# The complex sums and the way back of a spectral layer: sums over 128 partitions on GpSimd, products of 64 rows

## The chip, the cores and the metric

The kernel runs on one core of a Trainium2 chip. The metric is the device time of one execution, in microseconds (us). Before the change three runs gave 786.98, 787.42 and 789.71 us; the median is 787.42. The engines are called as in the profile: PE (TensorE matmul), PEld (its weight loads), DVE (VectorE), ACT (ScalarE), POOL (GpSimd) and SP (the queue that issues the DMAs).

## The reference

```python
def _A_ref(x, w_r, w_i):                 # spectral layer, S = 2048, D = 512
    X = rfft2(x); X = X * (w_r + 1j * w_i)
    return irfft2(X, s=(S, D))
def _B_ref(u, ...):                      # long convolution along S
    K = 2 * einsum("dn,dnl->dl", C, exp(A * dt * pos)).real
    y = irfft(rfft(u, 2 * L) * rfft(K, 2 * L))[..., :L]
    return y + u * D_skip
x = A_x
x = x + _A_ref(_layernorm(x), A_w_r, A_w_i)
x = x + _B_ref(_layernorm(x), ...)
x = x + _A_ref(_layernorm(x), A_w_r, A_w_i)
x = x + _B_ref(_layernorm(x), ...)
```

Everything is float32. The spectral layer (A) is a two-dimensional Fourier transform, a product with complex weights for each frequency, and the transform back. Layer B is a convolution whose kernel K (the "series") doesn't depend on x.

## The kernel before, in words

The transforms are matmuls with constant tables. A row index of 2048 is split into 128 x 16, and the 16 groups of frequencies are the steps `q` of a layer A (function `layer_a`). The layer has three lists of steps:

- `spread` (first layer) or `spread_four` (second layer): layer norm, sums and differences of the columns, and the first stage of the transform along the rows. The result is `ZA`.
- `middle`, for t = 0 to 17: `forward(t)`, `weigh(t-1)` and `back(t-2)`.
- `end`: `fold` and `rows_back`, the transforms back along columns and rows and the residual addition.

The change lies in `middle`, and there in these operations of each `q`:

- `forward` (lines 493 to 518): 4 matmuls of 128 rows and 128 weight columns (L497 to L501) into one bank; ACT copies the bank to the tile `z` in four pieces (L507, L511), two small places of which POOL has cleared (L503, L504). SP issues the DMA of the weights `W` (L513), and POOL patches two columns of them (L515).
- `weigh`: for each of the two parts `pl` (real, imaginary) a bank `px` gets two matmuls of 64 weight columns side by side, one for each half `v` of the frequencies (recorded as L316, the helper `side_by_side`). DVE multiplies it with both parts of the weights into `m[pl]` (L527, 128x514). Then the complex sums: real part = m[0][re] - m[1][im] (L532), imaginary part = m[1][re] + m[0][im] (L533), each for the half `v` of 64 partitions by itself, written so that in `Y` the real part lies in partitions 0 to 63 and the imaginary part in 64 to 127, with `v` as an index along the row. The strings `YA` (first layer) and `YA2` (second) name the engine of each of the four sums; g is POOL, v is DVE. One addition of 2 columns follows (L534, on POOL in the first layer, on DVE in the second).
- `back`: 4 matmuls (L545) with 128 columns of `Y` as weights, for both `v` and both `oe` (odd and even columns), each summing over the 128 partitions, real and imaginary together, into one bank; ACT copies the bank to `U[0]` and `U[1]` (L548), one copy for each `oe`.

The tag `u` is a pool of two buffers of 16 KB per partition. In turn it holds the rows of x of the first layer (`here`), the two halves of `U`, and in `layer_b` the tiles `Y` and `V`. PSUM has 8 banks; while the first layer runs, 5 of them are shared by `forward`, `weigh` and `back` (tags `p1`, `p2`, `p3`), in the second layer they have 2, 3 and 3. The tag `w` (7 buffers of 2 KB) holds `z`, `m` and `Y`, and in the second layer also the weights `W`.

Beside the first layer A runs `kernel_time`, the making of the series for layer B: 64 half units, each with matmuls (L825, L835, L836, L839, L870), exponentials and sines on ACT (L800), three kinds of DVE work (L838, L857, L859) and a product on POOL (L821, L822). Its steps are woven into the lists of the first layer A and of layer B in shares given by `FILL`, by the order in the program. A scheduler then orders the instructions of each engine by a timeline of its own and fills the gaps, so the order on an engine isn't that of the program text, and a change of one part can move others. Each engine works through its list in order. The second layer A has no series work beside it: its `middle` runs alone.

In layer B the function `weigh` multiplies the transformed rows by the transformed series (L962) and sums with L974, mostly on POOL.

## Time and profile before

| what | value |
|---|---|
| median of the runs | 787.42 us |
| span of the profiled execution, first to last instruction | 781.1 us |
| what lies around the span, by the median | 6.3 us |
| mean granted TensorE clock | 0.934 |
| bytes moved by DMA | 80.64 MB, mean 103 GB/s |

The profile is of one execution and gives its span; a separate whole time of that execution isn't recorded, so the 6.3 us are the median less the span. A line of a view names the place in the code (L545), the engine, the operation, what it writes and reads (the names of tiles), the size, and the count. A matmul of 32-bit numbers has two records, and each has a weight load of its own; "128*64" ahead of a size is the shape of the part of the array that the matmul uses, rows * columns. "[1.09 <-DMA wt]" is idle time of the engine ahead of the instruction, in us, and what ended it.

### The profile page before, as it was taken

What the parts mean: (1) busy time and instruction counts of PE and PEld (TensorE: products, weight loads), DVE (VectorE), ACT (ScalarE), POOL (GpSimd) and SP (SyncE); (2) the same over time, 40 slices, a digit from 0 to 9 for tenths busy, and PEclk for the clock granted to TensorE, in tenths of its full rate; (3) what the DMA queues carried; (4) which work ended last, traced back from release to release, by engine and by line L of the source; (5) the groups of instructions that cost most, each with busy time, mean ns of one, the idle gap of its engine ahead of it and who ended that gap; (6) DMA issues with size and microseconds to landing.
All of it is one profiled execution on the core that took longest, in us unless ns stands there. A gap on an engine that the chain in (4) does not pass through costs nothing. (4 is left out here: it accounts for less than half of the span.)

```text
span 781.1 us, 18929 instructions
## 1 busy us (share of the span) xinstructions
PE 627.7 (80%) x7248; PEld 443.5 (57%) x7248; DVE 649.3 (83%) x1301; ACT 428.1 (55%) x919; POOL 404.9 (52%) x596
## 2 busy tenths in 40 slices
PE   3447888897867977998889887874899896989986
PEld 2336666665534543656365656654777663566766
DVE  7998748979998999769996997878578696889992
ACT  3433778854748765887568834323756336242312
POOL 3675876764825245721657266281055572475760
PEclk9998899999979997999989999997999999799998
DMA  8300552344546503452325539422133114234513
GB/s 311 128 0 1 129 138 56 110 75 151 114 167 184 137 9 64 124 145 82 51 68 117 192 55 257 141 95 69 55 82 83 28 28 136 70 95 120 154 29 83
DMA packets 144923, 80.64 MB, mean 103 GB/s; under 512 B 78561, under 2 KB 124513, under 8 KB 143937
## 3 DMA queue, kind: packets, MB, share of 16 engines
q1 hardware_dynamic: 144576, 78.90, 36.2%
q8 instruction: 58, 0.95, 0.5%
q0 software_dynamic: 256, 0.52, 0.4%
q14 instruction: 33, 0.26, 0.1%
HBM read 54.89 MB, written 25.03 MB: 102 GB/s over the span
## 5 line engine op out<-in xcount | busy, mean ns | idle before, releaser
L974 POOL TENSOR_TENSOR u<-wb,wb 64x512 f32<-64x512 f32 x90 | 129.2, 1436 | 85.2 <-DVE wb L962 75.9
L316 PE MATMUL p<-z,mb 128*64 128x512 f32 (+2 forms) x480 | 102.0, 535 | 8.3 <-DVE wb L962 5.4
L870 PE MATMUL pv<-qp 128*64 128x128 f32 x1024 | 78.9, 295 | 11.4 <-DVE qp L859 6.9
L859 DVE TENSOR_TENSOR qp<-qp,mag 128x1024 f32<-128x1024 f32 x64 | 83.8, 1317 | 1.0
L962 DVE TENSOR_TENSOR wb<-p,kk 128x512 f32<-128x512 f32 x128 | 80.6, 674 | 4.7 <-PE p L316 4.6
L870 PEld LDWEIGHTS pv<-qp 128*64 128x64 f32 x1024 | 62.0, 147 | 38.8 <-ACT stage L878 10.2
L648 ACT COPY z<-p 128x512 f32<-128x512 f32 x96 | 51.4, 597 | 58.1 <-PE p L316 43.7
L316 PE MATMUL p<-mb,u 128*64 128x64 f32 x2048 | 72.9, 235 | 10.6 <-DVE u L974 4.5
L316 PEld LDWEIGHTS p<-mb,u 128*64 128x64 f32 x2048 | 70.7, 150 | 18.7 <-issue 11.3
L857 DVE SCALAR_TENSOR_TENSOR qp<-qp,mag 128x256 f32<-128x256 f32 x128 | 64.8, 523 | 13.6 <-ACT qp L800 13.3
L654 DVE STREAM_TRANSPOSE z<-z 128x512 f32<-128x512 f32 x96 | 58.5, 673 | 18.0 <-ACT z L648 18.0
L527 DVE TENSOR_TENSOR w<-wt,p 128x514 f32<-128x514 f32 x64 | 42.6, 686 | 33.3 <-PE p L316 18.6
L1086 POOL TENSOR_SCALAR w<-w,norms 128x128 f32<-128x128 f32 x64 | 40.5, 647 | 51.9 <-DMA w<-h 28.3
L532 POOL TENSOR_TENSOR w<-w,w 64x257 f32<-64x257 f32 x48 | 40.1, 835 | 50.3 <-DVE w L527 46.2
L456 PE MATMUL p<-w,w 128*128 128x128 f32 x128 | 32.0, 429 | 40.8 <-DVE w L449 30.8
L987 ACT COPY u<-p 128x512 f32<-128x512 f32 x64 | 37.6, 590 | 43.8 <-PE p L316 43.8
L316 PEld LDWEIGHTS p<-z,mb 128*64 128x64 f32 x480 | 34.2, 140 | 37.0 <-issue 20.2
L456 PEld LDWEIGHTS p<-w,w 128*128 128x128 f32 x128 | 27.8, 318 | 44.7 <-issue 24.8
L800 ACT ACTIVATE kf<-pk 128x512 f32<-128x512 f32 x64 | 38.9, 608 | 24.1 <-PE pk L839 23.6
L316 PE MATMUL p<-t,w 64*64 64x128 f32 x1024 | 43.3, 290 | 5.8 <-issue 2.6
L974 DVE TENSOR_TENSOR u<-wb,wb 64x512 f32<-64x512 f32 x38 | 46.9, 1234 | 0.5
L800 ACT ACTIVATE qp<-kf,half 128x512 f32<-128x512 f32 x64 | 47.2, 737 | 0.1
(200 smaller groups left out, 1495.3 us busy)
## 6 DMA issues: line engine op xcount, KB each, us to landing
wt<-in_w SPq DMA_DIRECT2D x32, 257.0 KB
kf<-kk SPq DMA_DIRECT2D x32, 256.0 KB
kk<-kf SPq DMA_DIRECT2D x32, 256.0 KB
u<-in_x SPq DMA_DIRECT2D x16, 256.0 KB
hr<-in_x SPq DMA_DIRECT2D x16, 256.0 KB
kt<-stage SPq DMA_DIRECT2D x32, 128.0 KB
h<-hr SPq DMA_DIRECT2D x16, 256.0 KB
w<-kt SPq DMA_DIRECT2D x32, 128.0 KB
```

Of the source, the lines that this page charges most:

```text
L316: last = self.nc.tensor.matmul(out, weights, data, start=not more, stop=True, skip_group_check=True).ins
L456: nc.tensor.matmul(p[:, b], xf[:, b], t, start=True, stop=True)
L527: nc.vector.tensor_mul(m[pl], W, px[:, None, :].to_broadcast([128, 2, 257]))
L648: nc.scalar.copy(tiles["z"][:, :, :, b, m:m + 2].rearrange("p u j m r -> p (u j) (m r)"), ps[b].rearrange("p u j m r -> p (u j) (m r)"))
L654: nc.vector.transpose(tiles["zt"][:, u:u + 8].rearrange("p u j d -> p (u j d)"), tiles["z"][:, u:u + 8].rearrange("p u j b m r -> p (u j b ...
L800: last["x"] = nc.scalar.activation(*a, **k).ins
L857: nc.vector.scalar_tensor_tensor(QP[:, c, 0], QP[:, c, 1, :, ::-1], -1.0 if c else 1.0, m[:, 0], op0=ALU.mult, op1=ALU.mult)
L859: nc.vector.tensor_mul(t, t, mag[:, None, 1:3, 256 * j:256 * j + 256].to_broadcast([128, 2, 2, 256]))
L870: nc.tensor.matmul(p[64 * t:64 * t + 64, g], QP[:, c, 2, d:d + 2].rearrange("p s a -> p (s a)"), QP[:, c, 0:2, d:d + 2].rearrange("p k s b ...
L962: nc.vector.tensor_mul(split(m[c, pl], "du", [32, 16]), by_channel(p), split(k[c], "du", [32, 16]))
L974: self.added = e[0].tensor_sub(y[0:64], v[0, 0], v[1, 1]), e[1].tensor_add(y[64:128], v[0, 1], v[1, 0])
L1086: (self.nc.gpsimd if XNE[k] == "g" else self.nc.vector).tensor_scalar(t[:, k], t[:, k], scale, bias, op0=ALU.mult, op1=ALU.add)
```

## The change

The sums run over all 128 partitions: `Y` now has the half `v` in the partitions, as `m` has it, and real and imaginary part side by side along the row. That makes two sums of 128x257 in place of four of 64x257, both on POOL in both layers. Since real and imaginary part are no longer in different partitions, `back` sums them by two matmuls of 64 rows that accumulate (`r` = 0 and 1), for each half `v` and each `oe`: 8 matmuls in place of 4, the two halves into two banks. ACT copies one bank for each `v`. The table `ST` for `back` is twice as long, so the constant tile `ca` has 256 columns more. `U`, `here`, and `Y` with `V`, each become one tile of 32 KB, and the tag `u` one buffer.

```diff
-YA = 'ggvg'
+YA = 'gg'
...
-YA2 = 'gvgv'
+YA2 = 'gg'
...
-    ca.append(MM.transpose(2, 3, 0, 1, 4).reshape(128, 256))
+    ca.append(np.broadcast_to(MM.transpose(3, 0, 2, 1, 4).reshape(64, 512), (2, 64, 512)).reshape(128, 512))
...
-        here = [self.sb("u", [8, 512]) for _ in range(2)] if x is None else []
+        here = self.sb("u", [16, 512]) if x is None else None
...
             Y = self.sb("w", [2, 257])
-            for v in range(2):
-                hs = slice(64 * v, 64 * v + 64)
-                e = [nc.vector if c == "v" else nc.gpsimd for c in ya[2 * v:2 * v + 2]]
-                e[0].tensor_sub(Y[0:64, v], m[0][hs, 0], m[1][hs, 1])
-                e[1].tensor_add(Y[64:128, v], m[1][hs, 0], m[0][hs, 1])
+            e = [adders[c] for c in ya]
+            e[0].tensor_sub(Y[:, 0], m[0][:, 0], m[1][:, 1])
+            e[1].tensor_add(Y[:, 1], m[1][:, 0], m[0][:, 1])
             adders[ye].tensor_add(Y[:, :, 128], Y[:, :, 128], Y[:, :, 256])
...
-                U.extend(self.sb("u", [2, 16, 16, 8]) for oe in range(2))
-            p = self.ps("p3", [2, 2, 128])
+                u = self.sb("u", [2, 2, 16, 16, 8])
+                U.extend((u[:, 0], u[:, 1], u))
+            p = [self.ps("p3", [2, 128]) for v in range(2)]
+            for oe in range(2):
+                for r in range(2):
+                    for v in range(2):
+                        hs = slice(64 * v, 64 * v + 64)
+                        nc.tensor.matmul(p[v][:, oe], Y[hs, r, 128 * oe:128 * oe + 128], k["ST"][hs, int(q + v > 0), r],
+                                         start=r == 0, stop=r == 1, skip_group_check=True)
             for v in range(2):
-                st = k["ST"][:, int(q + v > 0)]
-                for oe in range(2):
-                    nc.tensor.matmul(p[:, oe, v], Y[:, v, 128 * oe:128 * oe + 128], st, start=True, stop=True,
-                                     skip_group_check=True)
-            for oe in range(2):
-                nc.scalar.copy(U[oe].rearrange("p s n q (v c) -> p v (s n) q c", v=2)[:, :, :, q],
-                               p[:, oe].rearrange("p v (n c) -> p v n c", c=4))
+                nc.scalar.copy(U[2].rearrange("p o s n q (v c) -> p v o (s n) q c", v=2)[:, v, :, :, q],
+                               p[v].rearrange("p o (n c) -> p o n c", c=4))
...
-        Y, V = self.sb("u", [2, 32, 64]), self.sb("u", [32, 2, 2, 32])
+        YV = self.sb("u", [2, 4096])
+        Y, V = split(YV[:, 0], "abc", [2, 32, 64]), split(YV[:, 1], "abcd", [32, 2, 2, 32])
...
-                    net.phase("a", x=(32768, 1), ta=(8192, 1), ca=(6912, 1), u=(16384, 2), w=(2056, WA), wt=(2056, WT), hr="wt",
+                    net.phase("a", x=(32768, 1), ta=(8192, 1), ca=(7704, 1), u=(32768, 1), w=(2056, WA), wt=(2056, WT), hr="wt",
...
-            outer.enter_context(net.phase("b", t2=(8192, 1), u=(16384, 2), kk=(2048, 8), ta="t2", wt="w", wb="w", xw="w"))
+            outer.enter_context(net.phase("b", t2=(8192, 1), u=(32768, 1), kk=(2048, 8), ta="t2", wt="w", wb="w", xw="w"))
```

In the changed kernel the sums are lines 530 and 531, the small addition is line 532 and the matmuls of `back` are still line 545; behind `layer_b`'s first lines every line number is one higher.

More of the change, by code (lines that the diff above doesn't have):

```diff
@@ L393, in consts @@
         def consts():
-            C = self.load("ca", "ca", [CUTS[-1] + 512])
+            C = self.load("ca", "ca", [CUTS[-1] + 768])
             k["R"], k["Q"] = ([C[:, a:b] for a, b in zip(CUTS[i:i + 4], CUTS[i + 1:i + 5])] for i in (0, 4))
             k["S"] = split(C[:, CUTS[-1]:CUTS[-1] + 256], "abc", [2, 2, 64])
-            k["ST"] = split(C[:, CUTS[-1] + 256:CUTS[-1] + 512], "ab", [2, 128])
+            k["ST"] = split(C[:, CUTS[-1] + 256:CUTS[-1] + 768], "abc", [2, 2, 128])
         if x is not None:
@@ L419, in spread @@
                 G = starts[starts.index(n2) + 1] - n2
-                norm["rows"] = [row(k_, here[k_ // 8][:, k_ % 8]) for k_ in range(n2, n2 + G)]
+                norm["rows"] = [row(k_, here[:, k_]) for k_ in range(n2, n2 + G)]
                 if not S1:
@@ L1160, in switch @@
                 banks.enter_context(net.phase("pb", P, p1=(2048, PB[0]), p2=(2048, PB[1]), p3="p1"))
-                outer.enter_context(net.phase("h", side="right", za=(32768, 1), ca=(6912, 1), wv="kk", junk="kk"))
+                outer.enter_context(net.phase("h", side="right", za=(32768, 1), ca=(7704, 1), wv="kk", junk="kk"))
                 wide.enter_context(net.phase("wide", side="right", wb=(2048, WW), z3=(16384, 1), xw=(2048, 4)))
```

## The prediction

> I call the 16 steps of `middle` in the first spectral layer **Middle 1** (77 to 155 us) and those of the second **Middle 2** (561 to 616 us). A step holds one `forward`, one `weigh` and one `back`.
>
> **What bounds the kernel now.** First the page's busy times, then the busy time by stage (start and end, length, then busy us and instruction records of PE, PEld, DVE, ACT and POOL, granted clock, DMA share, GB/s).
>
> ```profile
> span 781.1 us, 18929 instructions
> PE 627.7 (80%) x7248; PEld 443.5 (57%) x7248; DVE 649.3 (83%) x1301; ACT 428.1 (55%) x919; POOL 404.9 (52%) x596
> ```
>
> ```profile
> 77.00:155.00 78.00, 67.20 (x505) 49.77 (x503) 57.78 (x82) 64.12 (x140) 55.75 (x116) 0.91 0.42 108
> 155.00:300.00 145.00, 118.53 (x1023) 71.39 (x1019) 129.75 (x294) 93.86 (x181) 72.66 (x101) 0.93 0.44 115
> 561.00:616.00 55.00, 50.76 (x384) 38.32 (x384) 40.91 (x80) 32.44 (x96) 28.53 (x74) 1.00 0.26 69
> ```
>
> No engine is the bound everywhere. In Middle 1 PE is busiest (67.2 of 78 us); from 155 to 300 us it is DVE (129.75 of 145); in Middle 2 it is PE again (50.76 of 55), with POOL at half. The weight loads in order of time show what one step of Middle 2 is made of.
>
> ```profile
> 589.78 0.30 PEld L497 LDWEIGHTS p<-ca,z 128*128 128x128 f32 x2 [0.39 <-issue]
> 590.67 0.97 PEld L545 LDWEIGHTS p<-ca,w 128*128 128x128 f32 x8
> 591.76 0.63 PEld L316 LDWEIGHTS p<-w,ca 128*64 128x64 f32 x8
> 592.78 0.30 PEld L497 LDWEIGHTS p<-ca,z 128*128 128x128 f32 x2 [0.39 <-issue]
> ```
>
> The step is 3.00 us long: 0.89 for `forward` (4 matmuls, 0.222 each), 1.09 for `back`, 1.02 for `weigh`, and PE waits for no engine in it. So Middle 2 is worth 16 x 3.0 = 48 us plus its beginning, its end and two stalls. `back` has 4 matmuls of the same form as `forward`, so about 0.88 of its 1.09 is streaming, and 0.21 is lost where the array goes over from 128*128 to 128*64. `weigh` has two pairs of matmuls of 257 columns, the halves of a pair side by side: `forward`'s columns (132, then three times 128) take 1.72 ns each, so 2 x 257 take 0.88, which leaves 0.14 for the way back to 128*128. **A change of the array's shape costs about 0.18 us.**
>
> By the Trainium skill, page "TensorEngine Tiling (Array Packing)", section "Key Properties", a change of tiling mode drains the engine. That speaks against this change, which brings in a third shape; the page has no price, and the 0.14 and 0.21 above agree with it.
>
> **The sums go to GpSimd.** The groups by line and shape (count, busy us, mean ns; the idle time is not needed) price the old and the new sums.
>
> ```profile
> L532 POOL TENSOR_TENSOR w<-w,w 64x257 f32<-64x257 f32 x48 | 40.1, 835 | 50.3 <-DVE w L527 46.2 <-ACT kf L800 1.6 <-ACT w L511 0.7
> L533 POOL TENSOR_TENSOR w<-w,w 64x257 f32<-64x257 f32 x32 | 21.4, 669 | 2.3
> L533 DVE TENSOR_TENSOR w<-w,w 64x257 f32<-64x257 f32 x32 | 18.8, 587 | 1.1
> L532 DVE TENSOR_TENSOR w<-w,w 64x257 f32<-64x257 f32 x16 | 10.3, 644 | 1.5 <-DVE w L527 0.5
> L1062 POOL TENSOR_TENSOR t<-za 128x512 f32<-128x512 f32 x8 | 11.1, 1419 | 0.1
> L974 POOL TENSOR_TENSOR u<-wb,wb 64x512 f32<-64x512 f32 x90 | 129.2, 1436 | 85.2 <-DVE wb L962 75.9 <-DVE wb L964 4.0
> L588 POOL TENSOR_TENSOR wv<-w 128x254 f32<-128x254 f32 x32 | 26.3, 823 | 0.8
> ```
>
> POOL takes as long for 128 rows as for 64 (1419 and 1436 ns at 512 columns), so a 128x257 sum is priced by the 128x254 row, 0.82 us; the ends are the 64x257 means, 0.67 and 0.84. DVE loses 16 sums of 0.644 in Middle 1 (10.3 us) and 32 of 0.587 in Middle 2 (18.8 us). POOL goes from 48 sums to 32 in Middle 1 and keeps 32 in Middle 2. Does the new pair of POOL sums delay Middle 2, where the adds ran on DVE beside them?
>
> ```profile
> 590.74 0.68 DVE L527 TENSOR_TENSOR w<-wt,p 128x514 f32<-128x514 f32 x1
> 591.46 1.35 DVE L533 TENSOR_TENSOR w<-w,w 64x257 f32<-64x257 f32 x2
> 591.70 0.23 POOL L515 COPY wt<-ends 128x4 f32<-128x4 f32 x1 [1.09 <-DMA wt<-in_w]
> 591.89 1.42 POOL L532 TENSOR_TENSOR w<-w,w 64x257 f32<-64x257 f32 x2
> ```
>
> The products are ready at 591.42. POOL's queue first holds the patch of the next weights (L515), which waits for their DMA; now both sums are behind it, not only the subtractions. From 591.89 two sums of 0.82 end at 593.5, and the 128x2 addition on DVE about 0.2 later, 593.7: that is when `back` is due in the old rhythm (590.67 + 3.00). So it fits exactly, and if PE's step becomes longer there is slack. DVE's 18.8 us in Middle 2 buys nothing, for DVE wasn't late; without the cover of a longer step each 0.1 us of delay would cost 16 x 0.1 = 1.6 us.
>
> **The way back as 64-row products.** Per step 8 matmuls of 64 rows x 128 columns take the place of 4 of 128 rows. Before has no 64x128 shape; the nearest is 64*64 in layer B.
>
> ```profile
> 686.02 0.86 PEld L316 LDWEIGHTS p<-t,x 64*64 64x64 f32 x32
> ```
>
> 32 records in 0.86 us are 0.027 each, against 0.111 for a record of 128*128 (two records to a matmul): four quarters of the array run at once, two of them row halves. So a 64-row product alone takes 0.22 us like a full one, and one of rows 0 to 63 with one of rows 64 to 127 takes 0.22 together. The source alternates the halves, which would be 4 slots of 0.22 per step, as now. But the scheduler's order in the changed kernel often doesn't alternate: in steps 3, 5, 7, 9 and 11 of Middle 2 it issues one upper-half product, a matmul of `forward`, then three upper and four lower; in steps 4, 6, 8, 10 and 12 one upper, a matmul of `forward`, and then lower and upper in turn. If a product starts no earlier than the one ahead of it in the queue, and each half runs one at a time, the 128 products of Middle 2 need 88 slots, where 64 are needed now, and those of Middle 1 86. The shape changes go from 34 to 66 in Middle 2 and from 44 to 73 in Middle 1, counted in the same two orders.
>
> Middle 2: 24 more slots x 0.22 = 5.3 us, 32 more changes x 0.18 = 5.8 us, together 11.1 us. Bounds: 0 if halves always overlap and the new changes are free; 64 x 0.22 + 32 x 0.20 = 20.5 if they never overlap.
>
> By the Trainium skill, page "TensorE: Matmul & The Clock Gate", section "Part 3: Packing small matmuls", matmuls start and end in program order; by that rule it is the 88 slots, while halves pulled forward past each other would make it 64 and the sum 5.3 us less. No row of before shows a run of one half followed by a run of the other.
>
> **What comes back.** Two steps of Middle 2 are longer than 3.00 because POOL's patch came late.
>
> ```profile
> 579.19 0.30 PEld L497 LDWEIGHTS p<-ca,z 128*128 128x128 f32 x2 [0.39 <-issue]
> ...
> 583.77 0.30 PEld L497 LDWEIGHTS p<-ca,z 128*128 128x128 f32 x2 [0.39 <-issue]
> ...
> 598.78 0.30 PEld L497 LDWEIGHTS p<-ca,z 128*128 128x128 f32 x2 [0.39 <-issue]
> ...
> 602.79 0.30 PEld L497 LDWEIGHTS p<-ca,z 128*128 128x128 f32 x2 [0.39 <-issue]
> ```
>
> They took 4.58 and 4.01 us, 2.6 more than two plain steps. With steps of about 3.7 us the weights have more time; I take 2.1 of the 2.6 as won. **Middle 2: 11.1 - 2.1 = +9.0 us.**
>
> **Middle 1 and the kernel's time series behind it.** Here `middle` is woven with units of `kernel_time`, whose DVE work is
>
> ```profile
> L859 DVE TENSOR_TENSOR qp<-qp,mag 128x1024 f32<-128x1024 f32 x64 | 83.8, 1317 | 1.0
> L857 DVE SCALAR_TENSOR_TENSOR qp<-qp,mag 128x256 f32<-128x256 f32 x128 | 64.8, 523 | 13.6 <-ACT qp L800 13.3
> L838 DVE TENSOR_SCALAR kw<-pk 128x512 bf16<-128x512 f32 x64 | 43.0, 677 | 1.7 <-PE pk L836 1.6
> ```
>
> 0.68 + 2 x 0.52 + 1.32 = 3.0 us for each of 64 half units. PE gets 22 slots x 0.22 + 29 changes x 0.18 = 10.1 us more, at the clock of 0.91 that this stage was granted 11.0 us, as much as all its idle time there (78 - 67.2 = 10.8). DVE gets 10.3 us less. The scheduler also moves series work back: at the end of Middle 1 DVE has done 4 half units where it had done 6, at the first `weigh` of layer B 24 where it had done 30; by that layer's 32nd weighting product both have 51, and from there to Middle 2 the orders are nearly the same. So if DVE sets the pace up to there, the stretch ends 10.3 us earlier; if PE does, 11.0 later. The rows above say PE for the first 78 us and DVE for the 145 behind it, and the half units that leave Middle 1 go to where DVE has little room (15 us in 145). What held DVE in Middle 1 is partly relieved:
>
> (waits from 80 to 152 us: total, times, longest)
>
> ```profile
> DVE w L527 <- POOL w L534: 8.8, 2, 6.1
> DVE w L527 <- PE p L316: 5.3, 4, 1.8
> ```
>
> but the longest of those waits, 6.1 us, is the 128x2 addition on POOL behind a series instruction that waits for ACT,
>
> ```profile
> 112.40 0.24 POOL L821 TENSOR_TENSOR e<-mag 128x16 f32<-128x16 f32 x1 [2.90 <-ACT mag L800]
> ```
>
> and in the changed kernel an L821 still stands ahead of that addition in the same step. The ends nearly cancel; I take **+1.0 us**, ends -10 and +11.
>
> **At no cost:**
>
> ```profile
> L548 ACT COPY u<-p 128x256 f32<-128x256 f32 x64 | 20.7, 374 | 9.7 <-PE p L545 9.6
> 17.63 0.33 SPq L305 DMA_DIRECT2D ca<-in_ca  x1
> 73.21 0.81 PE L497 MATMUL p<-ca,x 128*128 128x132 f32 x2 [0.46 <-ACT x L458]
> ```
>
> ACT's two copies per step keep their 256 elements; the 0.13 MB more of `ca` (256 columns x 128 rows x 4 bytes) are asked for at 18 us and needed at 73; the one 32 KB buffer makes `back`'s first write wait for all rows of the layer, and layer B's first write for all of the folds, both of which stand ahead in the data flow anyway. `back` takes two banks instead of one: with steps of 3 us or more its copies (0.37 us each) free them in time. From 616 us to the end the order is unchanged.
>
> **Sum.** 781.1 + 9.0 + 1.0 = 791.1 us of span. The median of the runs, 787.42, is 6.3 above the span, which I leave as it is: 797.4 us.
>
> **Rivals.**
> 1. *No overlap of the halves at all:* each runs alone. Middle 2 then costs 20.5 - 2.6 = 17.9, Middle 1 half of 64 x 0.22 + 29 x 0.20 = 20, so 10: 815 us. Against it: the 64*64 row.
> 2. *It cancels:* DVE's 10.3 us come off up to layer B, for it is the busiest engine behind Middle 1, and Middle 2 costs the 9.0: 786 us.
> 3. *Faster:* PE takes row halves without a drain and overlaps them whatever their order. Middle 2 then keeps its 3.0 us step (-1 for the stalls), and DVE's 10.3 us up to layer B lead, of which I count 8: 778 us. It decides if a change to 64*128 costs under 0.05 us and a step needs no more than 4.3 slots. Against it: the 0.21 behind every `back` now.
> 4. *GpSimd becomes the bound:* if a 128-row sum took twice a 64-row one, 1.43 us, POOL would need 2.9 and 0.2 for the patch per step, 3.1, still less than PE's 3.7: it adds nothing unless rival 3 holds. The L1062 row is against it.
>
> **Chances.** The forecast 0.66, rival 1 0.09, rival 2 0.14, rival 3 with 4 0.11. A measurement of this kernel tells apart about 0.5%, 3.9 us: faster 0.11, same 0.14, slower 0.75. The forecast's own range is 789 to 806: 7 either way for Middle 1, short of its ends, and 32 x 0.04 for the price of a shape change. For 8 in 10 it has to reach rival 2 and some way to rival 1: 785 to 810.
>
> **What would show it.** Middle 2's step by its L497 starts: 3.2 where the halves alternate, about 3.8 and 4.2 in the two other orders; all at 3.0 means rival 3, all above 4.3 rival 1. POOL's 128x257 near 0.8 us. L527 on DVE in Middle 2 waiting for PE, and PE for nobody. The 32nd L962 of layer B within some 5 us of its old time; 10 earlier would mean rival 2. I am wrong if PE waits for POOL in Middle 2, or if the series work shifts the stretch up to 300 us by more than 11.

## The result, and the profile after

The changed kernel takes **820.75 us** in the median of four runs (811.35 to 822.92), the kernel before 788.21 us beside it: a ratio of 1.041, 95% interval 1.034 to 1.048. It is slower, as forecast, but by 32 us, where 10 were forecast, and lies above the range of 785 to 810.

The page's busy times of the changed kernel, and the windows of the two stages ahead of 300 us and of the new Middle 2:

```profile
span 820.8 us, 19319 instructions
PE 654.5 (80%) x7504; PEld 457.4 (56%) x7504; DVE 619.0 (75%) x1253; ACT 430.1 (52%) x919; POOL 380.0 (46%) x580
```

```profile
77.00:155.00 78.00, 73.69 (x615) 52.77 (x612) 45.97 (x63) 58.98 (x132) 39.22 (x98) 0.93 0.41 107
155.00:300.00 145.00, 115.54 (x952) 68.80 (x951) 120.33 (x284) 83.82 (x163) 65.09 (x94) 0.87 0.42 112
589.00:652.00 63.00, 59.43 (x496) 43.81 (x496) 22.42 (x47) 32.99 (x96) 23.61 (x73) 1.00 0.22 60
```

From 77 to 155 us PE is busy for 73.69 us instead of 67.20, DVE for 45.97 instead of 57.78: more for PE and less for DVE, as the sum had it. Over the whole span PE is busy 27 us longer, DVE 30 us less. But from 155 to 300 us DVE, the bound of that stage before, does 9.4 us less work than before, and no engine does more. Work has been put off.

Where it went is seen in the first and last start of four groups of DVE instructions (their columns: count, shortest, median and longest ns, first and last start). L859 ends each half unit of the series; L601 is the residual addition that ends the first layer A; L962 (after: L963) is layer B's weighting; L527 in the second layer marks Middle 2. Before:

```profile
L601 DVE TENSOR_TENSOR hr<-hr,p x16: 647/672/687, 164.4 to 229.2; 128x512 f32<-128x512 f32 x16
L962 DVE TENSOR_TENSOR wb<-p,kk x64: 650/672/692, 284.5 to 517.0; 128x512 f32<-128x512 f32 x64
L859 DVE TENSOR_TENSOR qp<-qp,mag x64: 1185/1218/2301, 126.8 to 454.5; 128x1024 f32<-128x1024 f32 x64
L527 DVE TENSOR_TENSOR w<-wt,p x32: 681/690/692, 564.4 to 612.1; 128x514 f32<-128x514 f32 x32
```

After:

```profile
L601 DVE TENSOR_TENSOR hr<-hr,p x16: 653/677/689, 162.8 to 224.8; 128x512 f32<-128x512 f32 x16
L963 DVE TENSOR_TENSOR wb<-p,kk x64: 656/673/692, 280.8 to 544.4; 128x512 f32<-128x512 f32 x64
L859 DVE TENSOR_TENSOR qp<-qp,mag x64: 1202/1224/2152, 133.6 to 481.7; 128x1024 f32<-128x1024 f32 x64
L527 DVE TENSOR_TENSOR w<-wt,p x32: 681/691/694, 592.6 to 650.8; 128x514 f32<-128x514 f32 x32
```

The first layer A ends 4.4 us *earlier* and layer B's weighting begins 3.7 us earlier, but the series ends 27.2 us later, and Middle 2 begins 28.2 us later. The distance from the end of the series to Middle 2 is the same (109.9 and 110.9): **in these two kernels the series is the chain that everything up to Middle 2 hangs on.** Middle 2, from its first to its last start of L527, lasts 58.2 us instead of 47.7, and from there to the end it is 170.0 us instead of 169.0. So of the two terms of the forecast, Middle 2 (+9.0) came out at about +10, and the other (+1.0) at over twenty.

In every profiled run from here on but one, the whole time stands 1.7 to 1.9 us above the span (2.3 in e6). The 6.3 us that the prediction took for what lies around the span were thus mostly the distance of one quick execution from the median: by this, before's own profiled execution took some 783 us, an estimate, for its time isn't recorded. Three later kernels (e2, e11, e12 below), which leave the first layer and the series as they were, begin Middle 2 at 569.2, 571.0 and 569.2 us; against these 569.8 the changed kernel is 22.8 us late, and with Middle 2's 10 this makes the 32 of the medians.

### The profile page after: what moved, and what is told of

Read it like the earlier page. It is cut to its first block, busy times and chain, and to the rows that moved or that the text cites. A ratio compares the mean times of both kernels' runs of the same rounds, so it can differ in the third digit from the quotient of the medians.

```text
span 820.8 us, 19319 instructions
## 1 busy us (share of the span) xinstructions
PE 654.5 (80%) x7504; PEld 457.4 (56%) x7504; DVE 619.0 (75%) x1253; ACT 430.1 (52%) x919; POOL 380.0 (46%) x580
## 5 line engine op out<-in xcount | busy, mean ns | idle before, releaser
L316 PE MATMUL p<-z,mb 128*64 128x512 f32 (+1 forms) x480 | 102.8, 537 | 11.8 <-DVE wb L963 8.8
L870 PE MATMUL pv<-qp 128*64 128x128 f32 x1024 | 81.3, 302 | 12.4 <-DVE qp L859 7.2
L963 DVE TENSOR_TENSOR wb<-p,kk 128x512 f32<-128x512 f32 x128 | 80.8, 675 | 4.0 <-PE p L316 3.9
L859 DVE TENSOR_TENSOR qp<-qp,mag 128x1024 f32<-128x1024 f32 x64 | 81.0, 1268 | 1.2
L316 PEld LDWEIGHTS p<-mb,u 128*64 128x64 f32 x2048 | 69.9, 149 | 18.6 <-issue 11.0
L316 PE MATMUL p<-mb,u 128*64 128x64 f32 x2048 | 71.7, 234 | 10.5 <-DVE u L975 4.3
L857 DVE SCALAR_TENSOR_TENSOR qp<-qp,mag 128x256 f32<-128x256 f32 x128 | 64.8, 524 | 14.0 <-ACT qp L800 13.3
L654 DVE STREAM_TRANSPOSE z<-z 128x512 f32<-128x512 f32 x96 | 58.5, 674 | 20.6 <-ACT z L648 20.6
L527 DVE TENSOR_TENSOR w<-wt,p 128x514 f32<-128x514 f32 x64 | 41.8, 687 | 36.2 <-PE p L316 23.0
L545 PE MATMUL p<-ca,w 64*128 64x128 f32 x512 | 53.9, 299 | 5.9 <-POOL w L532 2.7
L838 DVE TENSOR_SCALAR kw<-pk 128x512 bf16<-128x512 f32 x64 | 43.2, 679 | 16.7 <-PE pk L836 16.5
L545 PEld LDWEIGHTS p<-ca,w 64*128 64x128 f32 x512 | 43.0, 193 | 18.1 <-POOL w L530 4.9
L530 POOL TENSOR_TENSOR w<-w,w 128x257 f32<-128x257 f32 x32 | 23.0, 719 | 64.7 <-DVE w L527 62.7
```

The source lines that it names most:

```text
L316: last = self.nc.tensor.matmul(out, weights, data, start=not more, stop=True, skip_group_check=True).ins
L527: nc.vector.tensor_mul(m[pl], W, px[:, None, :].to_broadcast([128, 2, 257]))
L545: nc.tensor.matmul(p[v][:, oe], Y[hs, r, 128 * oe:128 * oe + 128], k["ST"][hs, int(q + v > 0), r], start=r == 0, stop=r == 1, skip_group_c ...
L654: nc.vector.transpose(tiles["zt"][:, u:u + 8].rearrange("p u j d -> p (u j d)"), tiles["z"][:, u:u + 8].rearrange("p u j b m r -> p (u j b ...
L838: nc.vector.tensor_scalar(whole, p, MAGIC, -MAGIC, op0=ALU.add, op1=ALU.add)
L857: nc.vector.scalar_tensor_tensor(QP[:, c, 0], QP[:, c, 1, :, ::-1], -1.0 if c else 1.0, m[:, 0], op0=ALU.mult, op1=ALU.mult)
```

## The experiments

The column "us" holds medians; "ratio" is that to the kernel before on the same chip. "64th" is the start of the last L859, which ends the series. The counts say how many of its 64 half units stand in DVE's list ahead of the last L601 and of the first weighting of layer B. The columns between are read from one profiled execution of each kernel.

| kernel | counts | first layer A ends | 64th | Middle 2 begins | lasts | us | ratio (95%) |
|---|---|---|---|---|---|---|---|
| before | 19, 30 | 229.2 | 454.5 | 564.4 | 47.7 | 788.21 | 1 |
| after | 16, 24 | 224.8 | 481.7 | 592.6 | 58.2 | 820.75 | 1.041 (1.034 to 1.048) |
| e1 | 16, 24 | 228.7 | 485.6 | 596.7 | 48.0 | 812.94 | 1.030 (1.024 to 1.035) |
| e2 | 19, 30 | 232.2 | 459.3 | 569.2 | 58.1 | 797.53 | 1.011 (1.006 to 1.016) |
| e3 | 16, 24 | 220.1 | 473.1 | 585.0 | 46.7 | 802.91 | 1.016 (1.010 to 1.021) |
| e4 | 14, 24 | 211.8 | 474.0 | 586.7 | 58.0 | 819.49 | 1.036 (1.030 to 1.041) |
| e5 | 14, 24 | 211.1 | 475.9 | 599.8 | 47.4 | 818.65 | 1.040 (two runs) |
| e6 | 20, 31 | 241.1 | 474.4 | 585.7 | 58.5 | 811.72 | 1.030 (1.024 to 1.035) |
| e7 | 22, 32 | 240.9 | 462.3 | 573.8 | 48.0 | 794.83 | 1.010 (1.006 to 1.014) |
| e8 | 27, 37 | 264.8 | 462.8 | 588.7 | 48.5 | 806.41 | 1.026 (1.020 to 1.032) |
| e9 | 20, 31 | 239.6 | 468.8 | 580.5 | 48.4 | 795.63 | 1.012 (1.007 to 1.017) |
| e10 | 16, 25 | 222.5 | 475.3 | 583.8 | 47.4 | 800.12 | 1.018 (1.012 to 1.025) |
| e11 | 19, 30 | 234.6 | 461.9 | 571.0 | 47.4 | 786.19 | 1.000 (0.997 to 1.004) |
| e12 | 19, 30 | 230.3 | 458.7 | 569.2 | 47.2 | 788.99 | 1.005 (1.001 to 1.009) |
| e13 | 14, 24 | 210.3 | 475.4 | 588.0 | 47.3 | 808.77 | 1.033 (1.028 to 1.037) |
| e14 | 16, 24 | 226.1 | 481.4 | 594.2 | 48.0 | 810.80 | 1.036 (1.030 to 1.041) |
| e15 | 16, 25 | 222.1 | 477.9 | 586.8 | 48.1 | 798.99 | 1.020 (1.016 to 1.025) |
| e16 | 19, 29 | 233.1 | 464.5 | 576.3 | 47.3 | 795.04 | 1.014 (1.009 to 1.019) |

The theories: **S**, the loss ahead of Middle 2 comes from the series' half units, which the scheduler has moved back; **P**, it is the price of the new instructions in the first layer itself; **B**, it comes from the one 32 KB buffer that layer B's `Y` and `V` now share. For Middle 2, that it pays for the order of the 64-row halves, with the weights' patch behind it (**W**).

### Which layer pays (e1, e2)

```diff
-YA2 = 'gg'                      # e1: second layer A (and layer B's buffers) as before
+YA2 = 'gvgv'
+NEW1, NEW2 = True, False        # e2: False, True, with YA = 'ggvg'
...
-            e[0].tensor_sub(Y[:, 0], m[0][:, 0], m[1][:, 1])
+            if new: ...         # sums, back, tables and buffers by layer
```

> The change in the first spectral layer alone; the second layer, and layer B's two 16 KB buffers, as before. Theory S (series order: the scheduler finishes the first layer earlier and puts 3 to 6 of the 64 half units of the series behind it, where each costs its full 4.5 us): this kernel has the same order up to the second layer as the changed kernel, so the second layer's middle starts 25 to 30 us late, its step is 3.0 us again, and the whole is 810 to 817 us. Theory P (the 64-row products make PE late in the first layer): the same total, so this run does not tell S from P. Rival B (the one 32 KB buffer under layer B's Y and V makes layer B late): about 788 to 795.

> The change in the second spectral layer alone, with layer B on the one 32 KB buffer; first layer as before. The series has the same order as in the kernel before. Theories S and P: only the second middle is longer, by 10 to 13 us, so 797 to 801 us. Rival B: layer B is late as well, 815 or more.

The first layer alone costs 25.1 us (812.94 against 787.86), the second alone 9.7 (797.53). Together they make 34.8, and the whole change had 32.5. e2 has the shared 32 KB buffer in layer B, and its Middle 2 begins like that of e11 and e12: B falls.

### The series moved back, by itself (e3)

The kernel before, with the shares that weave the series into the program changed so that the scheduler's list has the changed kernel's counts:

```diff
-FILL = [0.31, 0.45, 0.5, 0.69, 0.84, 0.99]
+FILL = [0.05, 0.20, 0.5, 0.69, 0.84, 0.99]
```

> The kernel before with nothing of the change; only the shares of the series that are woven into the first layer are cut from 0.31 and 0.45 to 0.05 and 0.20. On DVE this leaves the half units done at the end of the first layer at 16 (before 19, changed 16) and at the first weighting of layer B at 24 (before 30, changed 24), and 51 at the 32nd in all three. Theory S: the start of the second middle moves from 561 to 580 or later, and the whole is 805 to 818 us. Theory P: the series fits in behind as I had predicted, within 5 us of before, 784 to 793 us.

```profile
L601 DVE TENSOR_TENSOR hr<-hr,p x16: 652/675/689, 165.5 to 220.1; 128x512 f32<-128x512 f32 x16
L859 DVE TENSOR_TENSOR qp<-qp,mag x64: 1203/1218/2173, 127.2 to 473.1; 128x1024 f32<-128x1024 f32 x64
```

Not one instruction is changed, only their order, and the kernel is 15.0 us slower. The first layer ends 9 us earlier than before and the series 18.6 later (11 to 14 later than in e2, e11 and e12): the picture of the changed kernel. Six half units fewer stand ahead of the first weighting; at the 3.0 us of DVE that the prediction gave each, that is 18 us. Middle 2 begins where S had it, but the time is 2 us short of S's range of 805 to 818. So S is right for about 15 of e1's 25 us; some ten remain for P.

### The halves in turn (e4, e5)

The eight products of `back` are chained so that upper and lower half alternate, in both layers; in the second layer they also follow `forward`'s last matmul and come one step later.

```diff
+                        with ExitStack() as stack:
+                            if last is not None:
+                                stack.enter_context(self.tc.issue_after(last))
+                                stack.enter_context(self.tc.high_priority(20000))
...
-                            nc.tensor.matmul(p[v][:, oe], ...)
+                            last = nc.tensor.matmul(p[v][:, oe], ...).ins
```

> The changed kernel, but the eight products of a step are chained so that the halves alternate in both layers, and in the second layer they follow all four matmuls of forward. Both theories: the step of the second middle is 3.2 us throughout, 7 to 8 us less in all there. Theory S: the series is as late as in the changed kernel (14, 24 and 51 half units at the same three points), so the second middle starts at 585 to 595 and the whole is 808 to 816 us. Theory P: the first layer's PE loses about 5 us of slots and up to 4 of shape changes, and the second middle starts at 575 to 582, the whole 798 to 806.

The starts of the steps of e4's Middle 2, and four of its waits there (total us, times, longest):

```profile
602.06 0.30 PEld L497 LDWEIGHTS p<-ca,z 128*128 128x128 f32 x2 [0.39 <-issue]
605.26 0.30 PEld L497 LDWEIGHTS p<-ca,z 128*128 128x128 f32 x2 [0.39 <-issue]
609.37 0.30 PEld L497 LDWEIGHTS p<-ca,z 128*128 128x128 f32 x2 [0.39 <-issue]
613.53 0.30 PEld L497 LDWEIGHTS p<-ca,z 128*128 128x128 f32 x2 [0.39 <-issue]
```

```profile
POOL wt L515 <- DMA wt<-in_w: 30.1, 13, 2.8
ACT w L511 <- POOL w L503: 22.7, 14, 2.2
PE p L316 <- ACT w L511: 4.5, 9, 0.7
PEld p L550 <- POOL w L530: 3.5, 6, 1.6
```

The first steps take 3.20 us, as the order promises; from 605 us on they take 4.1, no less than in the changed kernel (4.13 and 3.81). Behind the saved slots stood another bound: POOL waits 13 times, 2.3 us in the mean, for weights that have not landed, and what is queued behind that patch is late too: the sums, for which PE's weight loads wait, and the clearing of `z` (L503), for which ACT waits 22.7 us and PE then waits for ACT. In the first layer the lighter `back` ends the layer 13 us earlier (211.8 against 224.8). The whole time is 1.3 us below the changed kernel's, which its spread doesn't tell from nothing, and above the ranges of both theories.

e5 gives the patch to DVE (`WE2 = 'v'`), and is e4 otherwise.

> Like the kernel with the products in turn, but in the second layer the weights' patch runs on DVE instead of POOL. In that kernel the step of the second middle is 3.2 us five times and then 4.1 to 4.2, with PE waiting for POOL and POOL for the weights' DMA (30 us in 13 waits). Theory W (the weights' DMA stands ahead of both sums in POOL's queue): with the patch off POOL the step is 3.2 to 3.4 us throughout, 8 to 10 us less, about 810 us. Rival (PE or the sums themselves need 4.1): no change, about 819 us.

```profile
608.81 0.30 PEld L497 LDWEIGHTS p<-ca,z 128*128 128x128 f32 x2 [0.39 <-issue]
612.01 0.30 PEld L497 LDWEIGHTS p<-ca,z 128*128 128x128 f32 x2 [0.39 <-issue]
615.21 0.30 PEld L497 LDWEIGHTS p<-ca,z 128*128 128x128 f32 x2 [0.39 <-issue]
```

```profile
DVE wt L515 <- issue: 13.0, 1, 13.0
```

The step is 3.20 now to the end and Middle 2 as short as before (47.4), but the kernel gained nothing: the first patch stands in DVE's list ahead of layer B's last transposes and weightings, where DVE sits 13.0 us at it, and Middle 2 begins 124 us behind the series instead of 109 to 113.

### The series moved forward (e6, e7, e8)

The scheduler put the series back in the changed kernel; can one put it forward? In all three the first product of `fold` is queued behind the series' latest product, and the shares are changed. e6 is the changed kernel with 0.14 and 0.36; e7 and e8 are the kernel before with 0.16, 0.40 and 0.31, 0.45.

```diff
-FILL = [0.31, 0.45, 0.5, 0.69, 0.84, 0.99]
+FILL = [0.14, 0.36, 0.5, 0.69, 0.84, 0.99]
...
+                if x is None:
+                    stack.enter_context(self.tc.issue_after(self.totaled))
                 nc.tensor.matmul(p[:, 0:256], u[1][1], k["Q"][1], ...)
```

> The changed kernel with the series forced ahead in the first layer: the first product of each fold is queued on PE behind the latest series product, and the shares are 0.14 and 0.36. On DVE 20 half units are done at the end of the first layer and 31 at the first weighting of layer B (changed 16 and 24, before 19 and 30). Theory S: the series sets the pace, so the second middle starts at 565 to 577 instead of 592.6 us and the whole is 800 to 808 us. Theory P (the 64-row products in the first layer): the series' order is not what costs, 815 to 822 us.

> The kernel before, nothing of the change, with the same forcing of the series and shares 0.16 and 0.40: 22 half units at the end of the first layer and 32 at the first weighting (before 19 and 30). Theory S: 1 to 3 half units of about 4.5 us come forward, 777 to 785 us. If the first layer's own end is as much the pace here as the series, no change, 785 to 792 us.

> As the kernel before it in this list, with the shares 0.31 and 0.45: 20 half units before the first residual row, 27 at the end of the first layer, 37 at the first weighting. Theory S: the series ends 20 us or more earlier if it runs at its own pace of about 44 us for eight half units from the start, and the whole is 765 to 780 us, unless the first layer's end, which is pushed back, takes its place: then 785 to 800 us.

S in the simple form that stood behind these numbers, that each half unit earlier is gained, is wrong. e7 has more half units ahead than before and is 7 us slower, e8 still more and is 18.6 slower: the first layer's end moves out, from 229.2 to 240.9 and 264.8 us, while the series ends no earlier.

```profile
L604 DVE TENSOR_TENSOR hr<-hr,p x16: 653/672/687, 209.0 to 264.8; 128x512 f32<-128x512 f32 x16
L862 DVE TENSOR_TENSOR qp<-qp,mag x64: 1182/1218/2290, 129.4 to 462.8; 128x1024 f32<-128x1024 f32 x64
```

(e8.) Here the series isn't the chain any more: layer B's first weighting comes at 318.8 us instead of 284.5, and Middle 2 begins 125.9 us behind the series. What holds in all 18 profiles is the distance from layer B's last weighting to Middle 2, 47.4 to 49.3 us. The first layer and the series compete for the same time, and of the orders tried here the old one is the best. e6 wins 9 us of the changed kernel's 32, in between the two expectations.

### PE's time alone, and the halves in the first layer (e10, e15, e9, e13, e14)

What made the scheduler move the series? e10 is the kernel before with added time on PE and nothing else: in the first layer's `back`, the two products of v = 0 are issued twice.

```diff
-                    nc.tensor.matmul(p[:, oe, v], ...)
+                    for again in range(2 if x is None and v < 1 else 1):
+                        nc.tensor.matmul(p[:, oe, v], ...)
```

> The kernel before, except that in the first layer `back` issues the two products of v = 0 twice, with the same operands into the same place: 32 more products of 128x128, about 0.30 us each by the trace, so 9.6 us more of PE and nothing more for GpSimd, DVE, ScalarE or the buffers. The scheduler, left to itself, then puts 4 half units ahead of the end of Middle 1, 16 ahead of the first layer's end and 25 ahead of the first weighting: almost the changed kernel's 4, 16 and 24, where before has 6, 19 and 30. Theory E (PE's added time alone makes the first layer's cost, by the plan and on the chip): as e1, 805 to 815, the 64th half unit at 478 to 488, PE over 34.5 us busy from 115 to 150. Rival Q (sums on GpSimd or the buffer carry the ten us between e3 and e1): only the order's share as in e3, 799 to 804, the 64th half unit near 473. Rival R (PE has room): 786 to 792.

Left to itself the scheduler moves the series as in the changed kernel, and e10 is 13.3 us slower (800.12 against 786.83). With e3 this closes S: added time on PE makes the scheduler put five half units behind the first weighting (25 ahead of it, not 30) where the changed kernel and e3 have six, and these orders cost 13 to 15 us. (The added products take 5.4 us by PE's busy time in L545 and L546, 28.9 us instead of 23.5; the 9.6 of the expectation is too much.) But it is Q's number: e1's other ten us aren't in it. e14 and e15 repeat e1 and e10 on one chip, with e13 beside them: the change in the first layer only, products in turn.

> The same kernel as e1, beside e13 and e15 on one chip, since the changed kernels spread over 1.3% from run to run. If the gap between e1 and e10 is real it stands again: 807 to 817, 6 to 14 us above e15. If it was spread: within 4 us of e15.

> The same kernel as e10 (old sums, two of four products of the first layer's `back` issued twice) beside e13 and e14 on one chip: 797 to 804 if e10 was no chance.

> The change in the first layer only, products of `back` in turn, the series left where the scheduler puts it (4, 14 and 24 half units ahead of the end of Middle 1, of the first layer and of the first weighting; e1 has 4, 16 and 24). Theory H (the ten us between e1 and the two kernels with old sums and the same series order, e3 and e10, are the order of the 64-row halves, which takes PE's last room): as e3 and e10, 798 to 804, first layer's end at 209 to 216 us. Rival N (with this series order the series sets the pace and the lighter PE only ends the first layer earlier): as e1, 807 to 815.

The gap stands: 810.80 against 798.99. The windows from 115 to 150 us, of e14, e15 and e13 in this order:

```profile
115.00:150.00 35.00, 34.99 (x316) 24.34 (x316) 24.09 (x37) 27.56 (x66) 19.03 (x45) 0.99 0.30 90
```

```profile
115.00:150.00 35.00, 33.22 (x283) 25.54 (x281) 27.65 (x43) 27.46 (x67) 21.82 (x52) 1.00 0.30 95
```

```profile
115.00:150.00 35.00, 33.76 (x336) 24.20 (x336) 26.20 (x41) 28.83 (x69) 17.59 (x40) 1.00 0.30 90
```

In e14 PE has no idle time left (34.99 of 35.00 us). I took this for P's cause, and e13 says that it is at most a small part: with the halves in turn PE has room again and the first layer ends 15.8 us earlier than in e14 (210.3 against 226.1), but the time falls by 2.0 us only, which the spread of either doesn't tell from nothing. That is rival N: at this order of the series the first layer's end sets little.

Where the ten us arise can be read from the traces. The next table takes the stretch from the first weighting of layer B to the 32nd, and counts the half units that DVE has left to do in it (51 stand ahead of the 32nd, 56 in e8):

| half units left | profiles | that stretch, us |
|---|---|---|
| 27 | after, e1, e3, e4, e5, e13, e14 | 142.0 to 144.6 |
| 26 | e10, e15 | 135.8, 138.7 |
| 22 | e16 | 126.4 |
| 21 | before, e2, e11, e12 | 117.0 to 118.3 |
| 20 | e6, e9 | 118.0, 117.3 |
| 19 | e7, e8 | 113.5, 114.1 |

The count sets the stretch, with old sums and new, and with one buffer `u` or two; in e3 nothing else was changed. The clock granted in it, from 0.85 to 0.92 among the seven kernels of the first row, moves it by no more than those 2.6 us. **From 21 to 27 half units it grows by 26 us, 4.3 for each, and not the 3.0 of DVE's work alone.**

So e10 and e15 weren't at e1's order after all: with one half unit less to do in it, their stretch is 8.1 us shorter than e1's and 4.9 shorter than e14's, the largest part of what separates their starts of Middle 2 (12.9 and 7.4 us). e3 has e1's order, but its first weighting comes at 276.0 us where e14 has 282.1 and e1 284.7; these 6 to 9 us are P, what the new first layer costs ahead of layer B, and e13, at 279.0, has half of them back. **Not settled** is the rest of P: the sums on GpSimd and the one 32 KB buffer of the first layer were never changed by themselves. Nor is layer B's last part, where e14 takes 3.9 us longer than e15 from the end of the series to Middle 2, and e1 2.6 longer than e10, with the same instructions; the granted clock differs there (0.87 and 0.91 in e14 and e15), but no run separates it.

e9 has both: the change in the first layer only, halves in turn, the series forward as in e6.

> The change in the first layer only, with its eight products of `back` chained so that the halves alternate, and the series moved forward as in e6 (20 half units ahead of the first layer's end, 31 ahead of layer B's first weighting; before has 19 and 30). The second layer is as before. Theory E (what the first layer pays beside the series order is PE's time): in e1 PE is busy 34.92 of 35 us from 115 to 150 and 29.56 of 30 from 150 to 180, against 32.33 and 26.25 before; the order in turn ended the first layer 13.0 us earlier in e4, so that the series can go forward without pushing the layer's end: first layer ends at 222 to 232 us, the 64th half unit at 452 to 462, the time 786 to 796. Rival Q (the price lies in the sums on GpSimd or the one 32 KB buffer, which the order of the products does not touch): e6 less the 8 to 10 us of the second layer, 801 to 805, the 64th half unit near 472.

795.63, inside theory E's range and below Q's, and 6 us below e6 less the second layer's 9.7 (802.0, on another chip); the 64th half unit at 468.8 and the layer's end at 239.6 miss E's ranges, so its way there isn't shown. By the ratios (1.012 and 1.010) it costs what the old sums cost with nearly the same order of the series (e7): at that order the new first layer with the halves in turn costs nothing beyond the order itself that the spread would show.

### Middle 2 put right, and all together (e11, e12, e16)

e11 is the change in the second layer only, with the halves in turn, and DVE patches the weights from the fourth step on, so that no patch stands in layer B's way. e12 gives only this patch to the kernel before.

```diff
-            e = copies[we]
+            e = copies[we if x is None or q < 3 else "v"]
```

> The change in the second layer only (as e2), with the products of `back` in turn and behind the forward products, and the patch of the weights on DVE from the fourth step on; the first three patches stay on GpSimd, so that none stands in DVE's queue ahead of layer B's last weightings, as it did in e5. Theory W (the order of the halves is what Middle 2 pays, and behind it the wait for GpSimd's patch of a weight just landed; e5 failed only by the place of the first patches): step 3.2 us throughout, Middle 2 46 to 49 us long, 110 to 113 us from the 64th half unit to its start, the time 785 to 790. Rival X (with GpSimd relieved of the patch, its sums or DVE's fuller queue take their place, or the tail of layer B grows again): step 3.6 or more, or start of Middle 2 over 118 us behind the series: 793 to 800.

> The kernel before with the patch of the second layer's weights on DVE from the fourth step on. Before, GpSimd waits 10 times for such a weight, 12.3 us in all, and the step grows from 3.2 to over 4 at two places; Middle 2 takes 47.8 us. If those waits reach PE: Middle 2 45 to 46.5 us long, the time 784 to 787. Rival: DVE, with 13 more copies of about 0.2 us, holds the steps up as much: 787 to 791.

The steps of e11 (L508 is its L497):

```profile
602.36 0.30 PEld L508 LDWEIGHTS p<-ca,z 128*128 128x128 f32 x2 [0.39 <-issue]
605.56 0.30 PEld L508 LDWEIGHTS p<-ca,z 128*128 128x128 f32 x2 [0.39 <-issue]
608.76 0.30 PEld L508 LDWEIGHTS p<-ca,z 128*128 128x128 f32 x2 [0.39 <-issue]
```

786.19 us against 786.83, ratio 0.997 to 1.004: with the order of the halves and the place of the patch put right, the second layer's part of the change costs nothing. Theory W is right; how much the patch would give without the order in turn wasn't tried. e12 gained nothing: Middle 2 is 0.5 us shorter, the time 2.2 above, so the rival was right that the stalls of the kernel before are not to be had this way.

e16 is the whole change with the halves in turn in both layers, the late patches, and the series nearly in its old place.

> The whole change in both layers, products in turn (in the second layer behind the forward products), patches of the second layer's weights on DVE from the fourth step on, and the series at 19, 29 and 33 half units ahead of the first layer's end, the first and the ninth weighting, where before has 19, 30 and 33. Theory: with the order of the halves, the patch and the series' place put right the whole change costs nothing: Middle 2 46 to 49 us long, 64th half unit at 452 to 462, the time 784 to 793. Rival: forcing the series' place costs what it cost with the old sums in e7 and with the new in e9 (both about 795), 793 to 800.

795.04 us: 26 below the changed kernel, and still some 11 above the kernel before beside it (ratio 1.014). Middle 2 is as before (47.3); what is left is ahead of it, with the series' end at 464.5 us. The number is the rival's: like e7 and e9 it has the forced order. How much of it the order makes and how much the first layer isn't separated. No version here beats the kernel before.

## Why the prediction was wrong, step by step

**Middle 2, +9.0: right in its steps, and in part by luck in its sum.** The starts of the steps in the changed kernel:

```profile
598.37 0.30 PEld L497 LDWEIGHTS p<-ca,z 128*128 128x128 f32 x2 [0.39 <-issue]
601.57 0.30 PEld L497 LDWEIGHTS p<-ca,z 128*128 128x128 f32 x2 [0.39 <-issue]
604.78 0.30 PEld L497 LDWEIGHTS p<-ca,z 128*128 128x128 f32 x2 [0.39 <-issue]
608.91 0.30 PEld L497 LDWEIGHTS p<-ca,z 128*128 128x128 f32 x2 [0.39 <-issue]
612.72 0.30 PEld L497 LDWEIGHTS p<-ca,z 128*128 128x128 f32 x2 [0.39 <-issue]
```

3.20 and 3.21 us where the halves alternate, 4.13 and 3.81 in the two other orders, where 3.2, 4.2 and 3.8 were forecast. The alternating step has one change of shape more than the old one of 3.00 and the same slots: a change costs 0.20 us, 0.18 by the estimate. By itself the second layer's part costs 9.7 us (e2), and e5 and e11 show that the order of the halves, and a patch that is in time, take it back. By the Trainium skill, page "TensorE: Matmul & The Clock Gate", section "Part 3: Packing small matmuls", matmuls start and end in program order; the 4.13 beside the 3.81 agree: both steps have the same products and the same five changes of shape, and the one with runs of one half is 0.32 us longer, since of halves that don't stand in turn the array takes no pair.

The steps don't make the whole sum. From the fourth start of L497 to the last (570.19 to 605.79 us before, 598.37 to 640.99 after) the changed kernel loses 7.0 us, the stalls that it wins included. The other 3.5 of Middle 2's 10.5 us come behind the last start:

```profile
605.79 0.30 PEld L497 LDWEIGHTS p<-ca,z 128*128 128x128 f32 x2 [0.39 <-issue]
```

```profile
640.99 0.30 PEld L497 LDWEIGHTS p<-ca,z 128*128 128x128 f32 x2 [0.39 <-issue]
645.20 0.19 POOL L515 COPY wt<-ends 128x4 f32<-128x4 f32 x1 [2.43 <-DMA wt<-in_w]
646.04 0.29 PEld L545 LDWEIGHTS p<-ca,w 64*128 64x128 f32 x2 [1.48 <-POOL w L530]
649.32 0.19 POOL L515 COPY wt<-ends 128x4 f32<-128x4 f32 x1 [2.44 <-DMA wt<-in_w]
```

(The first before, the others after.) There a step has no `forward` and is still 4.1 us long, for POOL waits for a weight that has not landed, with both sums behind it, and PE waits for the sums.

What I hadn't seen is this second bound just behind the first. The prediction took slack at POOL for granted once the step is longer; but POOL waits for the weights in the changed kernel too,

```profile
POOL wt L515 <- DMA wt<-in_w: 30.2, 13, 2.8
PE p L545 <- POOL w L530: 2.0, 2, 1.0
```

30.2 us where PE waits for it only 2.0, up to 652 us. So "PE for nobody" held up to the last steps and failed in them, a small case of the sign "if PE waits for POOL in Middle 2"; e4 shows that a quicker PE would have met it at once.

**GpSimd's sums: right that they don't bind by their own length, too dear in the price.**

```profile
L530 POOL TENSOR_TENSOR w<-w,w 128x257 f32<-128x257 f32 x32 | 23.0, 719 | 64.7 <-DVE w L527 62.7
L531 POOL TENSOR_TENSOR w<-w,w 128x257 f32<-128x257 f32 x32 | 22.7, 709 | 0.0
```

0.72 and 0.71 us in the mean, where 0.82 was taken from a 128x254 row: nearer to the lower end, the old 64x257 sum.

**Middle 1 and the series behind it, "I take +1.0, ends -10 and +11": this step failed.** It measured +25 (e1, ratio 1.030) and somewhat more in e14 (ratio 1.036). Three things were wrong in it.

- It set DVE's 10.3 us less against PE's 11.0 more as if they met. They lie in different stages: from 77 to 155 us PE set the pace and DVE had room (57.78 of 78 us), so that DVE's gain fell into idle time. e15, which adds time on PE and takes none from DVE, isn't slower than e14 but 12 us faster.
- It saw that the scheduler moves six half units from ahead of layer B's first weighting to behind it, and that DVE has little room there, but gave this no price, since "by that layer's 32nd weighting product both have 51". The same count at a later point says nothing of the time at which it is reached. A price was in the rows: 6 half units x 3.0 us of DVE = 18 us, and alone it measured 15.0 (e3). With it the sum would have been 791.1 + 18 + 6.3 = 815 us, as far as the terms given then go. That 18 lies so near to 15.0 is in part luck: the stretch in question grew by 26 us, 4.3 for each half unit, and e3 had some of it back because its first weighting came earlier (276.0 us instead of 284.5).
- It took the two ends of one trade, PE's time and DVE's, for the bounds of the whole step. The order of the series was a third term, and outside them.

e10 shows the cause of the order: added time on PE alone moves the series. The remaining ten us of the first layer were not in my sum either. The traces place most of them, in a later first weighting than e3's (6 to 9 us) and in one half unit more to do behind it than e10 and e15 have (5 to 8 us); the halves account for some two us of the time at most (e13), and what else makes the first weighting late isn't settled.

**What lies around the span, 6.3:** it is about 1.8. By this estimate the sum began from an execution some 4.5 us quicker than the median, so that the 6.3 was right as a correction and wrong by its name.

**The rivals.** Rival 1 (halves never overlap, 815 us) gave the nearest number for a wrong reason: the steps at 3.2 refute it. Rival 2 (DVE's time comes off) and rival 3 with 4 are refuted by e1 and by the steps. The test that I had named showed it at once: layer B's 32nd weighting, the second of each pair here, came 24 us late (425.4 us, 401.6 before, and 406.7 to 409.3 in e2, e11 and e12) where I gave it 5.

```profile
400.99 1.27 DVE L962 TENSOR_TENSOR wb<-p,kk 128x512 f32<-128x512 f32 x2
```

```profile
424.75 1.27 DVE L963 TENSOR_TENSOR wb<-p,kk 128x512 f32<-128x512 f32 x2
```

The other sign, a shift of the stretch up to 300 us, could not show it: at the first weighting the changed kernel was still 3.7 us ahead.

## What to carry to other kernels

Where a scheduler orders the work, compare the order of the long chain that runs beside the changed part, and price each piece that it puts off at no less than that chain's full work per piece (3.0 us of DVE here, where the stretch that took the pieces grew by 4.3 for each), less what the stretch ahead gains; that both orders meet again later doesn't give the time back. An engine's saved time counts only in the stage where that engine is last. And 64-row products are as cheap as full ones, but for the change of shape, only if the two halves stand in turn in PE's queue; when a step gets shorter so, look at what stands one place behind, here a weight's landing that a sum waited for in the same queue.

## What the hardware showed beside

- A sum of 128x257 on GpSimd has a median of 639 ns, no more than one of 64x257; but single ones are far longer. The longest stands beside one long DVE instruction with two inputs (POOL, then DVE):

```profile
81.11 3.08 POOL L530 TENSOR_TENSOR w<-w,w 128x257 f32<-128x257 f32 x1 [0.79 <-DVE w L527]
```

```profile
80.89 2.82 DVE L773 TENSOR_TENSOR val<-val,hp 128x2560 f32<-128x2560 f32 x1
```

  It ends 0.48 us behind the DVE instruction, and takes 2.44 us longer than the median. That fits POOL standing still while DVE runs; no run here separates it.
- Kernels with the same first layer and the same order of instructions there differ by up to 7 us at the start of Middle 2 (564.4 in the profile of before, 569.2 to 571.0 in e2, e11 and e12). A difference of a few us between two single profiles is no finding; the costs above rest on the medians, and what is read from single profiles is where they arise.
- Part of that spread goes with PE's granted clock. From 635 us, where Middle 2 ends in both, e13 and e15 run the same code; e13 was granted 0.93 there and takes 171.2 us, e15 0.97 and 165.4 us:

```profile
635.00:806.20 171.20, 146.70 (x2144) 104.47 (x2142) 133.38 (x261) 56.55 (x114) 88.72 (x96) 0.93 0.28 82
```

```profile
635.00:800.40 165.40, 141.55 (x2142) 100.33 (x2142) 133.13 (x261) 56.52 (x114) 88.40 (x95) 0.97 0.29 84
```

  In the kernel before, the mean clock of a whole execution doesn't tell its time: 776.45 us had 0.910, 791.59 us 0.923.
